# Three weight tiles and the second token mixing's constants, moved into and behind the first chunk of a channel MLP

## The chip, the cores and the metric

The kernel runs on one NeuronCore of a Trainium2 chip. The metric is the device time of one execution in microseconds (us). Times are compared as medians of several runs. The profile is of one further execution.

## What is computed

For 4 batches of 576 tokens with 512 features the reference chains three blocks, all in fp32:

```python
# 1. linear attention, 8 heads of 64
q_p, k_p = phi(q), phi(k)                 # exp(+-(x @ w_phi - max|x @ w_phi|)), 256 features
num = q_p @ (k_p.T @ v); den = q_p @ sum(k_p); x = num / (den + 1e-6)
# 2. first mixer: low-rank token mixing, then a channel MLP of 2048
u = x + (x.T @ U @ V).T                   # U is 576 x 32, V is 32 x 576
x = u + relu(u @ w_ch1) @ w_ch2
# 3. second mixer: token mixing through 256, then a channel MLP of 1536
u = x + (relu(x.T @ w_tok1) @ w_tok2).T
out = u + relu(u @ w_ch1b) @ w_ch2b
```

## The kernel before

Weights arrive as 64-bit floats. `load64` fetches one half of a weight tile (128 x 512) into a ring of raw buffers (L139) and turns it into fp32: two ScalarE activations (L144 for the top word, L145 for the low word) and two VectorE operations (L147 and L150) that put them together. `split` then makes a high part (L96, for these tiles on ScalarE) and a low part (L101, for these tiles on GpSimd). A matrix product is three matmuls: high by high, high by low and low by high (all recorded at L108). The converted half lives in a tile `w` with two buffers, and the low words in `r` with two, so at most two halves are in conversion at once.

The work runs in three stages. Stage A is the attention of all 16 head pairs (`rounds`), with the first mixer's token mixing (`tm0`, `tm1`, `tm2`) and the first 5 of the 16 hidden tiles of the first channel MLP (`ma_u`, `ma_h`, `ma_y`) woven in. Partial results go to DRAM as `uD` (the input of the MLP) and `sD` (the sum so far), in eight chunks of 288 tokens. Stage B takes up these chunks one after the other with the other 11 hidden tiles (`wB`, named b0 to b10, two halves each), and after every second chunk runs the second token mixing (`tokmix2`, with the constants `T1H`, `T1L`, `T2H`, `T2L`). Stage C is the last channel MLP.

`channel` does one chunk. For each hidden tile f, TensorE makes `hp_b` (12 matmuls, `h_tile`), `relu_split` reads it (L185 on ScalarE writes `hhb`, L186 on VectorE writes `hlb`), and `second` adds the product of tile f-1 into four accumulators `yb` (12 matmuls). So TensorE's order is hp 0, hp 1, y 0, hp 2, y 1, hp 3 and so on, and `hp_b` has two buffers.

The order on each engine is settled when the program is built: a scheduler walks the program in its written order with estimated times, and places on each engine's list what is ready, earlier text first. On the chip each engine works through its own list in order. `tc.issue_after(ins)` adds an order edge: of the instructions in its block, those on the engine of `ins` are placed behind it; instructions on other engines are not touched. SyncE (SP) issues all the DMAs.

Before the change, the text after stage A is: load and convert all 11 tiles b0 to b10, load and split the first chunk's input (`u0`, which lives in the space of `T2H` and `T2L`), load and convert the constants of the second token mixing, then the chunks. Tiles b0 to b6 have buffers of their own; b7 to b10 take the buffers of stage A's tiles.

Of the kernel before, what the change touches and what calls it, by code (L numbers as in the profile page):

```python
# [9 lines left out]
F32R = mybir.dt.float32r  # L10
# [9 lines left out]
P = 128  # L20
B = 4
H = 8
S = 576
D = 64
F = 128
# [3 lines left out]
NT = 5  # L29
# [3 lines left out]
NA = 5  # L33
# [2 lines left out]
CHUNKS = (256, 512, 512, 512, 512)  # L36
HM = 256
EARLY = 2


NF32 = 4
WARM = 8


KQB = 6
# [44 lines left out]
def body(ctx, tc, kq, vd, w_phi, U, V, wm1, wt1, wt2, wm2, out):  # L90
# [14 lines left out]
        sub(el, lo, src, f32(hi))  # L105

    def mm(o, l, r, start, stop):
        nc.tensor.matmul(o, l, r, start=start, stop=stop, skip_group_check=True)  # L108

    def group(o, pairs, first=True):  # L110
        n = len(pairs)
# [224 lines left out]
    def k3(g):  # L336
        kvT = a1.tile([P, 2, 2 * F], F32, tag="kvT", name=f"kvT{g}")
        cp("a", kvT, kvps.pop(g))
        tp = psx.tile([P, 4, P], F32, tag="x", name=f"kvt{g}")
        for j in range(2):  # L340
            for s in range(2):
                nc.tensor.transpose(tp[:, 2 * j + s, :], kvT[:, j, s * F : (s + 1) * F], ident)
        if g < NF32:
            KHs[g] = a2.tile([P, 4, P], F32, tag="KH", name=f"KH{g}")
            cp("a", KHs[g], tp)
            return
        KHs[g] = a2.tile([P, 4, P], F32R, tag="KH", name=f"KH{g}")
        KLs[g] = a2.tile([P, 4, P], F32R, tag="KL", name=f"KL{g}")
        split(tp, KHs[g], KLs[g], "a", "v")

    QT = ((0, 1, 4), (2, 3))
    QS = (slice(0, 320), slice(320, S))

# [23 lines left out]
    def q2(g, j, ch):  # L377
        nm = f"{g}_{j}_{ch}"
        n = QS[ch].stop - QS[ch].start
        eh, el = qe.pop((g, j, ch))  # L380
        ps = psx.tile([P, 512], F32, tag="x", name=f"nm{nm}")
        gr = [(KHs[g][:, 2 * j + s], eh[:, s]) for s in range(2)]
        if el is not None:
            gr += [(KLs[g][:, 2 * j + s], eh[:, s]) for s in range(2)]
            gr += [(KHs[g][:, 2 * j + s], el[:, s]) for s in range(2)]
        group(ps[:, :n], gr)
        if ch == 0:
            nds[g, j] = a1.tile([P, S], F32, tag=f"nd{j}", name=f"nd{g}_{j}")
        cp("a", nds[g, j][:, QS[ch]], ps[:, :n])
# [9 lines left out]
    def xr(g):  # L399
        pk = pks.pop(g)  # L400
        with tc.issue_after(subs[-1]):
            nc.vector.tensor_scalar_add(pk, pk, EPS)
        nc.vector.reciprocal(pk, pk)
        rD = drr.tile([2, S], F32, tag="rD", name=f"rD{g}")
        nc.sync.dma_start(rD.rearrange("a (p i) -> (a p) i", i=9), pk)
        rec = a1.tile([P, S], F32, tag="rec", name=f"rec{g}", bufs=RECB)
        nc.sync.dma_start(rec[0:D], rD[0:1].to_broadcast([D, S]))
        nc.sync.dma_start(rec[D:P], rD[1:2].to_broadcast([D, S]))
        recs[g] = rec

    def x1(g):
# [5 lines left out]
            for j, rows in enumerate((slice(0, D), slice(D, P))):  # L417
                nc.vector.tensor_mul(xTs[b][rows, hp, :], nds.pop((g, j))[rows], rec[rows])

    rps = {}  # L420

    def tm0(b, t):
        xT = xTs[b]
        if t == 0:
            rps[b] = psx.tile([P, C], F32, tag="x", name=f"rp{b}")
        rp = rps[b]
        r = P if t < 4 else D
        xp = psx.tile([P, C], F32, tag="x", name=f"xp{b}_{t}")
        for c in range(NC):
            nc.tensor.transpose(xp[:r, c * P : (c + 1) * P], xT[:, c, t * P : t * P + r], ident)  # L430
        xh = at2.tile([P, C], F32R, tag="xh", name=f"xh{b}_{t}")
        xl = at2.tile([P, C], F32R, tag="xl", name=f"xl{b}_{t}")
        split(xp[:r], xh[:r], xl[:r], "a", "v")
        us = US[:r, t].rearrange("p a r -> p (a r)")
        mm(rp, us, xh[:r], t == 0, False)
        mm(rp, us, xl[:r], False, t == NT - 1)

    def tm1(b):
        rh = at2.tile([P, C], F32R, tag="xh", name=f"rh{b}")
# [4 lines left out]
    def tm2(b, ch):  # L444
        rh, rl = rps[b]
        sl = slice(ch * N, (ch + 1) * N)
        xT = xTs[b]
        for c in range(NC):
            mp = psx.tile([P, 512], F32, tag="x", name=f"mp{b}_{ch}_{c}")
            cs = slice(c * P, (c + 1) * P)  # L450
            group(mp[:, :N], [(rh[:, cs], VS[:, sl]), (rl[:, cs], VS[:, sl])])
            nc.vector.tensor_add(xT[:, c, sl], mp[:, :N], xT[:, c, sl])
        nc.sync.dma_start(uD[2 * b + ch], xT[:, :, sl])
# [99 lines left out]
    psg = PB.enter_context(tc.tile_pool(name="psg", bufs=1, space=PSUM, reuse_waits="tile"))  # L553

    nB = NF1 - NA
    wB = [load_w(wrB[f], wm1, NA + f, f"b{f}", f) if f < NR else load_w(wring, wm1, NA + f, f"b{f}") for f in range(nB)]

    def channel(ws, uh, ul, res, o, nm, dst=None, pool=mlp):
        n = uh.shape[2]
        yp = [psy.tile([P, 512], F32, tag=f"y{c}", name=f"y{nm}_{c}") for c in range(NC)]  # L560
        nf = len(ws)

        def second(f, hh, hl):
            wh, wl = ws[f]
            for c in range(NC):
                g = [(w2(wh, c), hh), (w2(wh, c), hl), (w2(wl, c), hh)]
                for i, (l, r) in enumerate(g):
                    mm(yp[c][:, :n], l, r, f == 0 and i == 0, f == nf - 1 and i == 2)

        prev = None  # L570
        for f in range(nf):
            hp = h_tile(psh, ws[f], uh, ul, f"{nm}_{f}")
            hh, hl = h_pair(f, f"{nm}_{f}", pool, n)
            relu_split(hp[:, :n], hh, hl)
            if prev is not None:
                second(*prev)
            prev = (f, hh, hl)
        second(*prev)
        for c in range(NC):
            nc.vector.tensor_add(o[:, c], yp[c][:, :n], res[:, c])  # L580
            if dst is not None:
                nc.sync.dma_start(dst[:, c], o[:, c])

    def tokmix2(b, x2):
        gp = [psg.tile([P, C], F32, tag=f"g{j}", name=f"gp{b}_{j}") for j in range(2)]
        for t in range(NT):
            r = P if t < 4 else D
            xp = psh.tile([P, C], F32, tag="m", name=f"x2p{b}_{t}")
            for c in range(NC):
                nc.tensor.transpose(xp[:r, c * P : (c + 1) * P], x2[:, c, t * P : t * P + r], ident)  # L590
            xh = b2.tile([P, C], F32R, tag="xh", name=f"x2h{b}_{t}")
            xl = b2.tile([P, C], F32R, tag="xl", name=f"x2l{b}_{t}")
            split(xp[:r], xh[:r], xl[:r], "a", "v")
            for j in range(2):
                js = slice(j * P, (j + 1) * P)
                g = [(T1H[:r, t, js], xh[:r]), (T1H[:r, t, js], xl[:r]), (T1L[:r, t, js], xh[:r])]
                for i, (l, rr) in enumerate(g):
                    mm(gp[j], l, rr, t == 0 and i == 0, t == NT - 1 and i == 2)
        gh = bc.tile([P, 2, C], F32R, tag="gh", name=f"gh{b}")
        gl = bc.tile([P, 2, C], F32R, tag="gl", name=f"gl{b}")  # L600
        for j in range(2):
            relu_split(gp[j], gh[:, j], gl[:, j])
        for ch in range(2):
            sl = slice(ch * N, (ch + 1) * N)
            for c in range(NC):
                cs = slice(c * P, (c + 1) * P)
                mp = psy.tile([P, 512], F32, tag=f"y{c}", name=f"m2p{b}_{ch}_{c}")
                g = []
                for j in range(2):
                    g += [(gh[:, j, cs], T2H[:, j, sl]), (gh[:, j, cs], T2L[:, j, sl]), (gl[:, j, cs], T2H[:, j, sl])]  # L610
                group(mp[:, :N], g)
                nc.vector.tensor_add(x2[:, c, sl], mp[:, :N], x2[:, c, sl])
            nc.sync.dma_start(u2D[:, :, b * S + ch * N : b * S + (ch + 1) * N], x2[:, :, sl])
# [6 lines left out]

    u0 = load_u(uD[0], "b0_0", bc, ("T2H", "T2L"))

    T1H = bc.tile([P, NT, 256], F32R, name="T1H")
    T1L = bc.tile([P, NT, 256], F32R, name="T1L")
    for t in range(NT):
        w = load64(wt1[:, t], P, 256, f"t1_{t}")
        split(w, T1H[:, t], T1L[:, t], "v", "v")
    T2H = bc.tile([P, 2, S], F32R, tag="T2H", name="T2H")
    T2L = bc.tile([P, 2, S], F32R, tag="T2L", name="T2L")
    for j in range(2):  # L630
        for k in range(2):
            sl = slice(k * N, (k + 1) * N)
            w = load64(wt2[:, j, sl], P, N, f"t2_{j}_{k}")
            split(w, T2H[:, j, sl], T2L[:, j, sl], "v", "v")

    for b in range(B):
        x2 = b2.tile([P, NC, S], F32, tag="x2", name=f"x2_{b}", bufs=1)
        for ch in range(2):
            nm = f"b{b}_{ch}"
            i = 2 * b + ch  # L640
            _, uh, ul = load_u(uD[i], nm) if i else u0
            xc = x2[:, :, ch * N : (ch + 1) * N]
            nc.sync.dma_start(xc, sD[i])
            channel(wB, uh, ul, xc, xc, nm)
        tokmix2(b, x2)

    BX.close()
    AB.close()
# [275 lines left out]
```

## Time and profile before

| | |
|---|---|
| runs | 1079.35 us median of 3 (1077.38 to 1079.73) |
| the profiled execution | 1074.05 us, of which the span from first to last instruction is 1072.3 us |
| TensorE (PE) busy | 1021.4 us, 95% of the span |
| VectorE (DVE), ScalarE (ACT), GpSimd (POOL) busy | 670.5, 455.5 and 240.4 us |
| chain of work that ended last | PE 75%, DVE 11%, ACT 5%, issue 3%, DMA 3%, POOL 2% |

The chain is followed back from the last instruction, at each step to what released it. PE's busy time counts matmuls that overlap in its pipeline, so a stretch with PE fully busy is one in which matmuls follow each other without a hole, not one at the peak. PEclk is the TensorE clock that was granted, as a share of 2.4 GHz: 1.00 and 0.50 are its two levels, and numbers between them are stretches that hold both.

### The profile page before, as it was taken

How to read it: one execution, taken by the hardware profiler on the slowest of the kernel's cores; microseconds unless marked ns; L12 is line 12 of the kernel's file. 1: busy time of each engine (PE TensorE's matmuls, PEld its weight loads, DVE VectorE, ACT ScalarE, POOL GpSimd, SP SyncE). 2: the span in 40 equal slices, each digit the busy share in tenths (PEclk: the TensorE clock that was granted, in tenths of full speed). 3: DMA queues.
4: the chain of work that ended last, by engine and by line, in shares of the span. 5: the costliest groups of instructions: out<-in, count | busy, mean ns of one | idle time of the engine just before them, and what ended most of it. 6: DMA issues, size and time to landing. Idle time of an engine off the chain costs nothing.

```text
span 1072.3 us, 17821 instructions
## 1 busy us (share of the span) xinstructions
PE 1021.4 (95%) x6960; PEld 948.1 (88%) x6960; DVE 670.5 (63%) x1203; ACT 455.5 (42%) x1067; POOL 240.4 (22%) x186
## 2 busy tenths in 40 slices
PE   8988999899989897999999999999999999999998
PEld 6767899799879787999999999999798988989887
DVE  7888987998898598743223322326898773644533
ACT  6766666756565566532112111114674331312211
POOL 3316556545555234200000000002251000000000
PEclk9999999999999989999999999999999999999999
DMA  7542322232220487520200200111663021030201
GB/s 215 163 148 65 98 69 80 72 98 72 76 79 24 126 276 240 142 79 23 90 23 23 89 23 1 48 42 60 224 204 108 2 83 36 3 116 1 79 1 39
DMA packets 62340, 92.16 MB, mean 86 GB/s; under 512 B 14512, under 2 KB 42928, under 8 KB 62256
## 3 DMA queue, kind: packets, MB, share of 16 engines
q1 hardware_dynamic: 62256, 91.03, 27.0%
q8 instruction: 54, 0.88, 0.3%
q14 instruction: 30, 0.25, 0.1%
HBM read 71.99 MB, written 18.95 MB: 85 GB/s over the span
## 4 chain that ended last, share of the span: by engine, by line
PE 75%; DVE 11%; ACT 5%; issue 3%; DMA 3%; POOL 2%; SPq 0%; DVEq 0%; ACTq 0%; POOLq 0%
PE yc L108 14%; PE yb L108 12%; PE hp_b L108 12%; PE hp_a L108 4%; PE nm L108 4%; PE pp L108 4%; PE kvp L108 4%; PE yp L108 3%; PE vc L108 3%; PE zc L108 3%; PE xc L108 3%; PE gp L108 2%; PE m2p L108 2%; PE dT L361 1%; DMA raw_a<-in_wm_dram 1%
## 5 line engine op out<-in xcount | busy, mean ns | idle before, releaser
L186 DVE SCALAR_TENSOR_TENSOR hlb<-hp_b,hhb 128x288 fp32r<-128x288 f32 x88 | 40.0, 456 | 159.2 <-ACT hhb L185 159.2
L185 ACT ACTIVATE hhb<-hp_b 128x288 fp32r<-128x288 f32 x88 | 36.0, 409 | 202.7 <-PE hp_b L108 199.9
L108 PE MATMUL hp_b<-ulb,wh_b 128*128 128x288 f32 x352 | 104.2, 296 | 0.0
L108 PE MATMUL hp_b<-uhb,wl_b 128*128 128x288 f32 x352 | 104.2, 296 | 0.0
L108 PE MATMUL hp_b<-uhb,wh_b 128*128 128x288 f32 x352 | 104.1, 297 | 0.0
L108 PE MATMUL yb<-hlb,wh_b 128*128 128x288 f32 x352 | 98.3, 299 | 2.3 <-DVE hlb L186 2.1
L101 POOL TENSOR_TENSOR sl<-w_c,sh 128x256 fp32r<-128x256 f32 (+1 forms) x18 | 24.6, 1391 | 329.5 <-ACT sh L96 325.0
L108 PE MATMUL yb<-hhb,wl_b 128*128 128x288 f32 x352 | 97.8, 297 | 0.0
L108 PE MATMUL yc<-hlc,vh 128*128 128x512 f32 (+1 forms) x240 | 88.6, 373 | 0.0
L108 PE MATMUL yc<-hhc,vl 128*128 128x512 f32 (+1 forms) x240 | 88.3, 373 | 0.0
L108 PE MATMUL yc<-hhc,vh 128*128 128x512 f32 (+1 forms) x240 | 81.0, 373 | 0.0
L101 POOL TENSOR_TENSOR qel<-qe,qeh 128x640 fp32r<-128x640 f32 (+1 forms) x48 | 71.4, 1499 | 25.5 <-DVE qeh L98 14.7
L108 PE MATMUL yb<-hhb,wh_b 128*128 128x288 f32 x352 | 68.5, 298 | 4.1 <-ACT hhb L185 4.1
L108 PEld LDWEIGHTS yb<-hlb,wh_b 128*128 128x128 f32 x352 | 66.7, 189 | 3.6 <-DVE hlb L186 3.6
L108 PEld LDWEIGHTS hp_b<-uhb,wh_b 128*128 128x128 f32 x352 | 66.4, 189 | 1.2 <-PE gp L108 1.1
L108 PEld LDWEIGHTS yb<-hhb,wl_b 128*128 128x128 f32 x352 | 66.9, 190 | 0.0
L108 PEld LDWEIGHTS hp_b<-ulb,wh_b 128*128 128x128 f32 x352 | 66.5, 189 | 0.1
L108 PEld LDWEIGHTS hp_b<-uhb,wl_b 128*128 128x128 f32 x352 | 66.3, 188 | 0.0
L293 DVE TENSOR_REDUCE km<-pp 128x4 f32<-128x512 f32 x80 | 54.7, 684 | 14.7 <-PE pp L108 14.2
L101 POOL TENSOR_TENSOR kel<-ke,keh 128x512 fp32r<-128x512 f32 x36 | 48.8, 1366 | 62.4 <-ACT keh L96 60.9
L108 PEld LDWEIGHTS yb<-hhb,wh_b 128*128 128x128 f32 x352 | 54.3, 190 | 4.3 <-ACT hhb L185 4.3
L101 DVE TENSOR_TENSOR kd<-pp,km 128x512 f32<-128x512 f32 x80 | 54.5, 682 | 0.7
(247 smaller groups left out, 3052.1 us busy)
## 6 DMA issues: line engine op xcount, KB each, us to landing
raw_c<-in_wm_dram SPq DMA_DIRECT2D x24, 512.0 KB, 4.5
raw_b<-in_wm_dram SPq DMA_DIRECT2D x22, 512.0 KB, 4.8
kq<-in_kq_dram SPq DMA_DIRECT2D x80, 128.0 KB, 2.2
raw_a<-in_wm_dram SPq DMA_DIRECT2D x10, 512.0 KB, 4.1
rec<-rD SPq DMA_DIRECT2D x32, 144.0 KB, 3.2
uD<-xT SPq DMA_DIRECT2D x8, 576.0 KB, 3.4
sD<-xT SPq DMA_DIRECT2D x8, 576.0 KB, 4.9
x<-sD SPq DMA_DIRECT2D x8, 576.0 KB, 5.3
```

The lines of the kernel that those rows point to most:

```text
L101: return ENG[e].tensor_tensor(out=o, in0=a, in1=b, op=ALU.subtract)
L108: nc.tensor.matmul(o, l, r, start=start, stop=stop, skip_group_check=True)
L185: a = nc.scalar.activation(hh, hp, AF.Relu)
L186: v = nc.vector.scalar_tensor_tensor(out=hl, in0=hp, scalar=0.0, in1=f32(hh), op0=ALU.max, op1=ALU.subtract)
L293: nc.vector.tensor_reduce(out=m, in_=pv, op=ALU.max, axis=AX.X, apply_absolute_value=True)
L361: nc.tensor.transpose(tp[:, o : o + r], ds["q", g, t][:r, j, :], ident[:r, :r])
```

## The change

Tiles b0 to b7 (`READY = 8`) stand where all eleven stood, and their instructions on SP, the 16 loads, are ordered behind the last load of the last reciprocal (`rec`, in `xr`). Tiles b8, b9 and b10 are loaded and converted inside the first chunk: after `relu_split` of hidden tiles 0, 1 and 2, with their ScalarE and VectorE instructions ordered behind those two of that `relu_split`. The constants of the second token mixing are loaded and converted after the first chunk in the text. `keep` would add matmuls, but its two counts are 0, so it adds none.

```diff
+READY = 8
+KEEP_M = 0
+KEEP_Q = 0
...
+    def keep(o, n, behind):
+        r = US.rearrange("p t a r -> p (t a r)")
+        with tc.issue_after(behind):
+            for i in range(n):
+                mm(o, r[:, :P], r[:, :512], i == 0, i == n - 1)
...
-        nc.sync.dma_start(rec[D:P], rD[1:2].to_broadcast([D, S]))
+        recl[:] = [nc.sync.dma_start(rec[D:P], rD[1:2].to_broadcast([D, S])).ins]
...
-    wB = [load_w(wrB[f], wm1, NA + f, f"b{f}", f) if f < NR else load_w(wring, wm1, NA + f, f"b{f}") for f in range(nB)]
+    def load_b(f):
+        if f < NR:
+            return load_w(wrB[f], wm1, NA + f, f"b{f}", f)
+        return load_w(wring, wm1, NA + f, f"b{f}")
+
+    with tc.issue_after(recl[0]):
+        wB = [load_b(f) for f in range(READY)]
...
-        nf = len(ws)
+        nf = nB
...
-            relu_split(hp[:, :n], hh, hl)
+            a, v = relu_split(hp[:, :n], hh, hl)
+            if len(ws) < nB:
+                with tc.issue_after(a), tc.issue_after(v):
+                    ws.append(load_b(len(ws)))
...
-    T1H = bc.tile([P, NT, 256], F32R, name="T1H")
...
+    def mix2_consts():
+        T1H = bc.tile([P, NT, 256], F32R, name="T1H")
...
+        return T1H, T1L, T2H, T2L
...
             channel(wB, uh, ul, xc, xc, nm)
-        tokmix2(b, x2)
+            if i == 0:
+                T1H, T1L, T2H, T2L = mix2_consts()
+        tokmix2(b, x2, T1H, T1L, T2H, T2L)
```

## Rows read from the trace of the kernel before

**Rows 1.** Windows: length; busy of PE, PEld, DVE, ACT, POOL; PEclk, DMA share, GB/s.

```profile
420.00:423.00 3.00, 2.99 (x23) 2.74 (x21) 2.98 (x5) 1.72 (x4) 1.30 (x1) 1.00 0.69 222
423.00:427.10 4.10, 0.00 (x0) 0.00 (x0) 2.93 (x5) 2.74 (x7) 1.54 (x2) 0.77 0.85 265
427.10:432.95 5.85, 5.21 (x23) 4.86 (x24) 4.69 (x6) 3.78 (x7) 2.27 (x2) 0.58 0.73 222
432.95:700.00 267.05, 267.05 (x1947) 261.05 (x1947) 93.96 (x191) 60.34 (x127) 5.17 (x4) 1.00 0.18 55
```

**Rows 2.** Timeline of PE: start, us, instruction, idle time before it and its releaser.

```profile
427.10 1.33 PE L108 MATMUL yb<-hhb,wh_b 128*128 128x288 f32 x4 [4.11 <-ACT hhb L185]
429.07 0.61 PE L108 MATMUL yb<-hlb,wh_b 128*128 128x288 f32 x1 [0.64 <-DVE hlb L186]
...
433.16 0.29 PE L108 MATMUL yb<-hhb,wh_b 128*128 128x288 f32 x1
...
434.76 0.30 PE L108 MATMUL hp_b<-uhb,wh_b 128*128 128x288 f32 x1
```

**Rows 3.** Timeline of ACT around the first chunk's first relu.

```profile
422.45 0.62 ACT L96 CAST wh_b<-w_b 128x512 fp32r<-128x512 f32 x1 [1.03 <-DVE w_b L150]
...
426.62 0.43 ACT L185 ACTIVATE hhb<-hp_b 128x288 fp32r<-128x288 f32 x1
```

**Rows 4.** Timeline of DVE around the first chunk's first relu.

```profile
422.34 0.81 DVE L498 TENSOR_TENSOR xT<-yp,xT 128x288 f32<-128x288 f32 x2
...
427.00 1.65 DVE L150 SCALAR_TENSOR_TENSOR w_b<-raw_b,w_b 128x512 int32<-128x512 int32 x1
428.57 0.44 DVE L186 SCALAR_TENSOR_TENSOR hlb<-hp_b,hhb 128x288 fp32r<-128x288 f32 x1
```

**Rows 5.** Windows of the tile `w_b` alone: two DVE instructions are one half.

```profile
366.00:423.10 57.10, 30.93 (x32) 19.83 (x33) 21.51 (x15) 0.94 0.75 252
423.10:443.10 20.00, 13.09 (x12) 7.16 (x12) 8.98 (x7) 0.83 0.59 175
```

**Rows 6.** Tile `w_b`: count, ns min/median/max, first and last start.

```profile
L144 ACT ACTIVATE w_b<-raw_b x22: 654/668/688, 367.2 to 437.9; 128x512 f32<-128x512 f32 x22
...
L150 DVE SCALAR_TENSOR_TENSOR w_b<-raw_b,w_b x22: 675/692/1774, 369.7 to 439.3; 128x512 int32<-128x512 int32 x22
L96 ACT CAST wh_b<-w_b x22: 603/620/640, 371.5 to 441.1; 128x512 fp32r<-128x512 f32 x22
L101 POOL TENSOR_TENSOR wl_b<-w_b,wh_b x22: 1263/1292/2176, 372.2 to 441.8; 128x512 fp32r<-128x512 f32 x22
```

**Rows 7.** Tile `T1H`: its first use and its conversion.

```profile
L108 PE MATMUL gp<-x2h,T1H x40: 387/437/501, 497.7 to 766.0; 128*128 128x512 f32 x32, 64*128 64x512 f32 x8
...
L101 DVE TENSOR_TENSOR T1L<-w_t,T1H x5: 412/424/426, 444.2 to 450.0; 128x256 fp32r<-128x256 f32 x5
```

**Rows 8.** Tile `T2H`: its first use and its conversion.

```profile
L108 PE MATMUL m2p<-T2H,gh x64: 290/295/398, 511.0 to 779.6; 128*128 128x288 f32 x64
...
L101 DVE TENSOR_TENSOR T2L<-w_t,T2H x4: 447/450/451, 459.3 to 463.6; 128x288 fp32r<-128x288 f32 x4
```

**Rows 9.** Timeline of SP: loads of raw halves.

```profile
71.69 3.32 SPq L139 DMA_DIRECT2D raw_b<-in_wm_dram  x2
...
363.23 0.42 SPq L139 DMA_DIRECT2D raw_b<-in_wm_dram  x1
```

**Rows 10.** DMA issues: us to landing, of the loads issued at 362.18 and 363.23.

```profile
raw_b<-in_wm_dram SPq DMA_DIRECT2D x1, 512.0 KB, 5.0
...
raw_b<-in_wm_dram SPq DMA_DIRECT2D x1, 512.0 KB, 6.5
```

**Rows 11.** Timeline of ACT in the last token mixing of stage A.

```profile
369.38 1.27 ACT L145 ACTIVATE r_b<-raw_b 128x512 int32<-128x512 uint32 x2
370.56 1.06 ACT L96 CAST xh<-xp 128x512 fp32r<-128x512 f32 x2
```

**Rows 12.** Waits of PE from 385 to 420 us: total, times, longest.

```profile
PE yp L108 <- DVE hla L186: 1.2, 2, 0.9
```

More of the change, by code (lines that the diff above doesn't have):

```diff
@@ L107, in mm @@
     def mm(o, l, r, start, stop):
-        nc.tensor.matmul(o, l, r, start=start, stop=stop, skip_group_check=True)
+        return nc.tensor.matmul(o, l, r, start=start, stop=stop, skip_group_check=True)
+    def keep(o, n, behind):
[3 more added lines that the diff above has]
+                mm(o, r[:, :P], r[:, :512], i == 0, i == n - 1)
     def group(o, pairs, first=True):
@@ L341, in k3 @@
             for s in range(2):
-                nc.tensor.transpose(tp[:, 2 * j + s, :], kvT[:, j, s * F : (s + 1) * F], ident)
+                kvl[g] = nc.tensor.transpose(tp[:, 2 * j + s, :], kvT[:, j, s * F : (s + 1) * F], ident).ins
         if g < NF32:
@@ L349, in k3 @@
         split(tp, KHs[g], KLs[g], "a", "v")
+    kvl = {}
     QT = ((0, 1, 4), (2, 3))
@@ L381, in q2 @@
         ps = psx.tile([P, 512], F32, tag="x", name=f"nm{nm}")
+        if g == NF32 - 1 and j == 0 and ch == 0:
+            keep(ps, KEEP_Q, kvl[g])
         gr = [(KHs[g][:, 2 * j + s], eh[:, s]) for s in range(2)]
@@ L418, in x1 @@
                 nc.vector.tensor_mul(xTs[b][rows, hp, :], nds.pop((g, j))[rows], rec[rows])
-    rps = {}
+    rps, rpl, recl = {}, {}, []
     def tm0(b, t):
@@ L435, in tm0 @@
         mm(rp, us, xh[:r], t == 0, False)
-        mm(rp, us, xl[:r], False, t == NT - 1)
+        rpl[b] = mm(rp, us, xl[:r], False, t == NT - 1).ins
     def tm1(b):
@@ L450, in tm2 @@
             cs = slice(c * P, (c + 1) * P)
+            if c == 0 and ch == 0 and b == 0:
+                keep(mp, KEEP_M, rpl[b])
             group(mp[:, :N], [(rh[:, cs], VS[:, sl]), (rl[:, cs], VS[:, sl])])
@@ L582, in channel, with tokmix2 @@
                 nc.sync.dma_start(dst[:, c], o[:, c])
-    def tokmix2(b, x2):
+    def tokmix2(b, x2, T1H, T1L, T2H, T2L):
         gp = [psg.tile([P, C], F32, tag=f"g{j}", name=f"gp{b}_{j}") for j in range(2)]
@@ L621, in body @@
     u0 = load_u(uD[0], "b0_0", bc, ("T2H", "T2L"))
-    T1H = bc.tile([P, NT, 256], F32R, name="T1H")
[L624 to L634, printed above, removed]
+    def mix2_consts():
+        T1H = bc.tile([P, NT, 256], F32R, name="T1H")
+        T1L = bc.tile([P, NT, 256], F32R, name="T1L")
+        for t in range(NT):
+            w = load64(wt1[:, t], P, 256, f"t1_{t}")
+            split(w, T1H[:, t], T1L[:, t], "v", "v")
+        T2H = bc.tile([P, 2, S], F32R, tag="T2H", name="T2H")
+        T2L = bc.tile([P, 2, S], F32R, tag="T2L", name="T2L")
+        for j in range(2):
+            for k in range(2):
+                sl = slice(k * N, (k + 1) * N)
+                w = load64(wt2[:, j, sl], P, N, f"t2_{j}_{k}")
+                split(w, T2H[:, j, sl], T2L[:, j, sl], "v", "v")
+        return T1H, T1L, T2H, T2L
     for b in range(B):
```

## The prediction

> **What bounds the kernel now.** I read the page first: the end is set by TensorE's own stream, so a change counts only where it closes a hole in that stream or moves the granted clock. Then I looked for holes around the change with the windows. From 432.95 to 700 us PE is busy for the whole 267.05 us at clock 1.00 [rows 1]: whatever is moved into that stretch costs nothing as long as it opens no hole, and a microsecond gained before it moves everything behind it forward. Just before it lies the one place that the change touches. From 420 to 423 us PE is full, from 423.00 to 427.10 it does nothing, and from 427.10 to 432.95 it works at a mean clock of 0.58 [rows 1].
>
> The timeline tells what ends the hole. PE has made hp 0 and hp 1 of the first chunk and now needs `hhb` of tile 0: it waits 4.11 us for it, does four matmuls, and waits 0.64 us more for `hlb` [rows 2]. The relu itself takes 0.43 us on ACT and 0.44 us on DVE. It is late because of what stands ahead of it on the two lists: ACT starts it only at 426.62, DVE at 428.57, right behind an L150 of a weight half [rows 3, 4]. The windows of `w_b` alone say which halves these are: up to 423.1 us there are 32 DVE instructions, that is 16 halves, exactly b0 to b7; the other 6 halves, b8 to b10, follow in the next 20 us [rows 5]. So the first chunk's first relu stands behind conversions of b8 and b9, which no matmul needs for another 20 us.
>
> **The change, part by part.**
>
> *The relu's place.* With b8 ordered behind the relu of tile 0 on both engines, the last conversion left ahead of it on ACT is the cast of b7's second half. That cast runs from 422.45 to 423.07 [rows 3]; with its 0.43 us the relu then ends at 423.5. On DVE the list ahead ends with two additions of stage A, 422.34 to 423.15 [rows 4], so `hlb` can run from 423.5 to about 423.95. PE runs dry at 423.0 [rows 1], so I leave a hole of 0.5 us. The four matmuls that need `hhb` alone, 0.53 us at the pace of 12 in 1.60 us [rows 2], then cover the wait for `hlb`. Of 4.11 + 0.64 = 4.75 us of waiting, 4.2 us go. Bounds: all 4.75 go if the relu slips ahead of b7's cast; 2.9 go if two activations of b8, 0.67 us each [rows 6], still stood ahead. I take 4.2, because the order edge covers all ACT and DVE instructions of b8.
>
> *The clock.* After the hole, 24 matmuls run from 427.10 to the start of y 1 at 433.16 us, 6.06 us with the 0.64 us wait in them; the next 12, at clock 1.00, take 434.76 - 433.16 = 1.60 us [rows 2]. At that pace the 24 would take 3.2 us, so the lower level of the clock costs 6.06 - 0.64 - 3.2 = 2.2 us. The engine had been idle for 4.11 us before. With a hole of 0.5 us I expect the clock to stay up: the nearest row is a hole of 0.9 us between 385 and 420 us [rows 12], and from 420 to 423 the clock still stood at 1.00 [rows 1]. Bounds: 0 (it falls anyway) and 2.2; I take 2.2. Sum of both terms: 4.2 + 2.2 = 6.4 us.
>
> *b8 to b10 inside the chunk.* 6 halves, each with two activations (0.67 us each, taking L145 like L144) and a cast (0.62) on ACT, 1.29 us on POOL [rows 6] and two DVE operations of 1.0 us on average (44.0 us in 44 [rows 5]): 5.2 us from end to end, and a new one every 20 / 6 = 3.3 us [rows 5]. Started at 423.9, b8 is whole at 423.9 + 3.3 + 5.2 = 432.4, b9 at 439.0, b10 at 445.6, its first half at 442.3. A step of the chunk (12 matmuls of hp, 12 of y) takes 3.2 us at the pace above, so with y 0 at 423.5, hp 8 starts at 423.5 + 1.6 + 6 x 3.2 = 444.3, hp 9 at 447.5, hp 10 at 450.7. The least cover is that of b10's first half, 8.4 us. Cost nothing; if that cover were gone, PE would wait for b10 by what is missing. Their 6 loads carry no edge on SP and keep their place in the ring of raw buffers, since the order b0 to b10, then constants, is the old one.
>
> *The constants.* Nine pieces move behind the chunk in the text. Before, T1's last split started at 450.0 and its first use at 497.7; T2's at 463.6 and 511.0 [rows 7, 8]. Both have 47 us of cover. T2 had to wait for `u0`'s space before as well. A few us later costs nothing.
>
> *The edge behind `rec`.* Two raw loads were issued at 71.69, some 290 us before the others; the third of the others was issued at 363.23 [rows 9]. With the edge these two join the burst behind `rec`. By the ring of raw buffers they are the halves of b1 (13 halves are loaded before b0, and of every five the first two use the ring that stage A has too), so they become third and fourth. Rows give landings of 362.18 + 5.0 = 367.2 for the first and 363.23 + 6.5 = 369.7 for the third [rows 10], so 1.3 us apiece and about 371.0 for the fourth. The first ACT instruction on b1 is the second of the two L145 from 369.38, so near 370.0 [rows 11]: 0.3 us after landing. Behind it on ACT stand casts `xh` of the last token mixing, which PE waits for. Bounds: a loss of 2.3 us if b1 landed as late as the fifth (372.3), a gain of 0.6 us if that L145 moves behind the `xh` casts. I take 0. The Trainium skill ("DMA: Bandwidth & Descriptors", Rules for kernel authors) says to issue a transfer early and wait on it late, which speaks against this edit; by that rule the early issue hid something and the sum would be 6.4 - 2.3 = 4.1 us, against 6.4 by the rows.
>
> *Nothing:* `keep` with counts of 0, and `nf = nB`, which is the same 11.
>
> **From the profiled execution to the runs.** It took 1074.05 us, 1.75 us of it outside the span; 6.4 less is 1067.65. The median of the runs is 5.3 us above it, and I take the saving off the median: 1079.35 - 6.4 = **1073.0 us**. About 0.2%, 2.2 us, is what a measurement of this kernel can tell from no change.
>
> **Rivals.**
>
> *The relu waits for something else.* The constants' conversions carry no edge, and the scheduler could fill ACT and DVE with them, or with the second chunk's input, where b8 stood. For it: the relu was placed by estimated times, and these had it late. Against it: b8 to b10 come first in the ring of raw buffers, so the constants have no buffer before b8 is converted. The hole would stay: 1079 us.
>
> *Half the gain.* The clock falls all the same (4.2 us saved, 1075.2 us), with two activations of b8 ahead as well (2.9 saved, 1076.5 us), or b1 lands late (6.4 - 2.3 = 4.1 saved, 1075.3 us). For the first speaks that the clock was at its lower level behind the only long hole here, against it that the hole shrinks to an eighth.
>
> *A looser stage A.* With the two early loads gone, the scheduler places the casts of the last token mixing ahead of conversions. Four `xh` casts stand behind an L145 or L144 of 0.67 us there at most once each, so up to 2.7 us: 1070.3 us.
>
> *Slower: relus of the first chunk held up at every step.* Where conversions and relus were mixed in stage A, PE waited for a relu (`hla`) twice, by up to 0.9 us [rows 12]; the list of DVE also held L150s there, of 0.69 us at the median and up to 1.77 [rows 6]. If each of the 10 later relus of the chunk cost 0.9 us, that is 9 us against 6.4 gained: 1082.0 us. The sign turns at 0.64 us a step. Against it: b9's last halves and b10 were mixed with relus after 432.95 already, and PE shows no hole there [rows 1], as a relu has 3.2 us until its product is due. The Trainium skill ("SBUF — State Buffer", § SBUF: two separate sides) has VectorE operations with two SBUF inputs and GpSimd operations that read SBUF exclude each other for a whole instruction. By that rule each L150 that meets the POOL subtraction is 1.1 us longer; at 10 steps it would be 11 us lost and 1084 us. The trace agrees on the length (1.77 against 0.69), not on any wait of PE in this stretch.
>
> **How the numbers follow.** As forecast (1071 to 1074.5): 0.58. Half the gain: 0.15, of it 0.04 for late b1. Looser stage A: 0.08. Relu waits for something else: 0.11. Slower: 0.08, of it 0.03 at the longer price. Faster by over 0.2%: 0.58 + 0.15 + 0.08 = 0.81; same 0.11; slower 0.08. The range from 1069.5 to 1079.2 leaves out the slower case, half of the unchanged one and a little of the lower one, 0.17 in all.
>
> **What would show it.** Right: `hhb` of tile 0 on ACT right behind the 16th `wh_b` cast; PE's wait for it under 1 us; PEclk 1.00 from 420 to 440; the 17th to 22nd `wh_b` casts after it and before 450 us; no wait of hp 8 to hp 10; T1 and T2 done well before 490. Wrong: a wait of `yb` or `hp_b` in tiles 1 to 10, a fall of the clock near 425, `xh` casts of the last token mixing waiting for a raw load, or a span that moves by other than the sum because the scheduler rearranged stage A, where two loads left the list at 71.69.

## The result, and the profile after

The changed kernel takes 1068.47 us at the median of 7 runs (1065.8 to 1072.49), the kernel before 1079.73 us beside it (7 runs, 1075.58 to 1083.54): ratio 0.9908, 95% interval 0.9885 to 0.9931. A second comparison on another occasion gave 0.9926 (0.9905 to 0.9947). The forecast of faster holds; the forecast time of 1073.0 us is 4.5 us too long, and the measured one lies 1.0 us below the lower end of the range. One execution of the kernel before (1405.55 us) and one of the filled kernel below (2524.1 us) were disturbed and are left out of every time here. The profiled execution took 1067.35 us, its span 1065.6 us against 1072.3: 6.7 us less, close to the 6.4 of the sum. So two questions are left: whether these 6.7 us come from where the sum has them, and where the rest of the 9 to 11 us between the medians is.

The page of the changed kernel gives busy time with share of the span, and the chain that ended last, by engine:

```profile
PE 1020.9 (96%) x6960; PEld 947.8 (89%) x6960; DVE 668.1 (63%) x1203; ACT 455.7 (43%) x1067; POOL 239.3 (22%) x186
...
PE 70%; DVE 14%; ACT 5%; DMA 4%; issue 4%; POOL 2%; SPq 0%; DVEq 0%; POOLq 0%; ACTq 0%
```

The work is the same and PE is still the bound. The same four windows as [rows 1], of the changed kernel:

```profile
420.00:423.00 3.00, 3.00 (x25) 3.00 (x24) 1.96 (x6) 2.96 (x6) 1.30 (x1) 1.00 0.57 132
423.00:427.10 4.10, 4.10 (x33) 4.10 (x32) 2.66 (x6) 3.77 (x8) 2.33 (x2) 1.00 0.49 180
427.10:432.95 5.85, 5.85 (x46) 5.85 (x45) 4.43 (x5) 3.40 (x7) 1.86 (x3) 1.00 0.85 280
432.95:700.00 267.05, 266.52 (x1935) 259.58 (x1934) 91.95 (x189) 58.80 (x124) 3.81 (x3) 1.00 0.17 54
```

The stretch that had no matmul has 33, and the clock, 0.77 and 0.58 before, is 1.00. Only the last window is worse than in [rows 1]: PE lacks 0.53 us in it. The timelines of ACT and of DVE show the relu of tile 0 where the forecast put it, and three later relus, of tiles 4, 5 and 6, that are late:

```profile
420.04 0.63 ACT L100 CAST wh_b<-w_b 128x512 fp32r<-128x512 f32 x1 [1.96 <-DVE w_b L160]
420.56 0.41 ACT L195 ACTIVATE hhb<-hp_b 128x288 fp32r<-128x288 f32 x1
420.87 0.67 ACT L154 ACTIVATE w_b<-raw_b 128x512 f32<-128x512 f32 x1
...
436.25 0.41 ACT L195 ACTIVATE hhb<-hp_b 128x288 fp32r<-128x288 f32 x1
...
440.60 0.45 ACT L155 ACTIVATE r_t<-raw_t 128x256 int32<-128x256 uint32 x1 [1.35 <-DVE w_t L157]
440.95 0.42 ACT L154 ACTIVATE w_t<-raw_t 128x256 f32<-128x256 f32 x1
441.27 0.40 ACT L195 ACTIVATE hhb<-hp_b 128x288 fp32r<-128x288 f32 x1
```

```profile
421.00 0.46 DVE L196 SCALAR_TENSOR_TENSOR hlb<-hp_b,hhb 128x288 fp32r<-128x288 f32 x1 [0.27 <-ACT hhb L195]
...
433.40 1.32 DVE L157 SCALAR_TENSOR_TENSOR w_b<-w_b,r_b 128x512 int32<-128x512 int32 x1 [1.26 <-ACT w_b L154]
434.64 0.45 DVE L196 SCALAR_TENSOR_TENSOR hlb<-hp_b,hhb 128x288 fp32r<-128x288 f32 x1
...
436.54 1.73 DVE L160 SCALAR_TENSOR_TENSOR w_b<-raw_b,w_b 128x512 int32<-128x512 int32 x1
438.19 0.44 DVE L196 SCALAR_TENSOR_TENSOR hlb<-hp_b,hhb 128x288 fp32r<-128x288 f32 x1
439.28 1.29 DVE L157 SCALAR_TENSOR_TENSOR w_t<-w_t,r_t 128x256 int32<-128x256 int32 x1 [0.65 <-ACT w_t L154]
```

420.04 is the cast of b7's second half, the 16th of 22; `hhb` of tile 0 follows it, at 420.56 where [rows 3] have 426.62, and b8 follows `hhb`. Further down, `hlb` of tile 4 stands behind an L157 of b10, that of tile 5 behind an L160 of b10 that takes 1.73 us, and `hhb` of tile 6 behind two conversions of the constants, the first of which (L155) waits for the L157 from 439.28. PE's timeline shows what each does:

```profile
421.47 0.69 PE L112 MATMUL yb<-hhb,wh_b 128*128 128x288 f32 x4
422.00 0.29 PE L112 MATMUL yb<-hlb,wh_b 128*128 128x288 f32 x1
...
434.17 0.69 PE L112 MATMUL yb<-hhb,wh_b 128*128 128x288 f32 x4
435.14 0.40 PE L112 MATMUL yb<-hlb,wh_b 128*128 128x288 f32 x1 [0.29 <-DVE hlb L196]
...
437.91 0.68 PE L112 MATMUL yb<-hhb,wh_b 128*128 128x288 f32 x4
438.69 0.40 PE L112 MATMUL yb<-hlb,wh_b 128*128 128x288 f32 x1
...
441.72 0.80 PE L112 MATMUL yb<-hhb,wh_b 128*128 128x288 f32 x4
442.57 0.40 PE L112 MATMUL yb<-hlb,wh_b 128*128 128x288 f32 x1
```

Where [rows 2] have waits of 4.11 and 0.64 us, y 0 follows hp 1 with none, and its first `hlb` matmul starts 0.53 us after its first matmul. In y 4, y 5 and y 6 the same distance is 0.97, 0.78 and 0.85 us, and y 6 starts 0.39 us after the last hp matmul in place of 0.13. Matmuls overlap, so only one of these delays is listed as idle time; it is the distance between starts that tells the loss. From y 4 to y 5 and from y 5 to y 6 it is 3.74 and 3.81 us, where the kernel before takes 3.18 for a step.

For this reason all kernels below are compared by the starts of the same matmuls. The table is worked out from such starts in the PE timelines, plus that of `x1` on DVE (us, from "to mp" on each since the column before; the names are those of the experiments below; "last x1": first of the last two multiplications L431 of stage A; mp: first of the second half of the last token mixing of stage A, which is that of the last batch; hp 0, y 1: of the first chunk; gp: of the first batch; hpc: the first hidden tile of stage C, near 760; before_look are two more executions of the kernel before):

```
kernel            edge  last x1  to mp  to hp 0  to y 1  to gp  to hpc  to end
before             no    364.1   12.21   43.33   13.56   64.57  269.65  304.89
before_look_1      no    362.0   14.02   43.75   14.29   64.58  269.76  306.22
before_look_2      no    368.8   13.36   43.64   14.21   64.57  269.72  306.06
fill               no    363.2   12.67   42.68   12.64   67.70  269.81  304.90
no_rec_edge        no    361.9   13.66   42.63    7.08   66.47  269.83  306.11
no_rec_again       no    364.5   13.51   42.60    7.11   66.73  269.77  306.09
all_eleven_ahead   yes   362.7   14.03   42.08   13.03   64.56  269.80  306.01
text_only          yes   362.9   13.79   41.78   13.25   64.56  270.13  306.05
after              yes   362.8   13.66   41.83    6.37   66.21  269.81  304.91
after_again        yes   362.3   12.52   41.80    6.37   66.30  269.78  304.89
consts_edge        yes   366.5   14.08   42.02    6.37   65.54  269.92  304.94
ready6             yes   361.6   14.00   41.78    6.37   69.21  269.69  304.97
xh_first           yes   370.8   12.60   45.62    6.37   65.71  269.64  306.15
```

From hp 0 to y 1 the change saves 13.56 - 6.37 = 7.19 us; from y 1 to gp it gives 1.64 us back. Ahead of hp 0 it saves 1.33 us (419.61 to 418.28); from gp on, nothing.

### The profile page after: what moved, and what is told of

It reads as the page before. It is cut to its first block, busy times and chain, and to the rows that moved or that the text cites. A ratio compares the mean times of both kernels' runs of the same rounds, so it can differ in the third digit from the quotient of the medians.

```text
span 1065.6 us, 17826 instructions
## 1 busy us (share of the span) xinstructions
PE 1020.9 (96%) x6960; PEld 947.8 (89%) x6960; DVE 668.1 (63%) x1203; ACT 455.7 (43%) x1067; POOL 239.3 (22%) x186
## 4 chain that ended last, share of the span: by engine, by line
PE 70%; DVE 14%; ACT 5%; DMA 4%; issue 4%; POOL 2%; SPq 0%; DVEq 0%; POOLq 0%; ACTq 0%
PE yc L112 14%; PE yb L112 11%; PE hp_b L112 11%; PE hp_a L112 4%; PE yp L112 3%; PE pp L112 3%; PE vc L112 3%; PE zc L112 3%; PE xc L112 3%; PE kvp L112 3%; PE gp L112 2%; PE nm L112 2%; PE m2p L112 2%; PE dT L372 2%; DVE xT L431 1%
## 5 line engine op out<-in xcount | busy, mean ns | idle before, releaser
L112 PEld LDWEIGHTS hp_b<-ulb,wh_b 128*128 128x128 f32 x352 | 66.2, 188 | 0.1
L112 PEld LDWEIGHTS yb<-hhb,wl_b 128*128 128x128 f32 x352 | 66.3, 188 | 0.0
L112 PEld LDWEIGHTS hp_b<-uhb,wl_b 128*128 128x128 f32 x352 | 66.2, 188 | 0.0
## 6 DMA issues: line engine op xcount, KB each, us to landing
uD<-xT SPq DMA_DIRECT2D x8, 576.0 KB, 3.5
sD<-xT SPq DMA_DIRECT2D x8, 576.0 KB, 5.0
x<-sD SPq DMA_DIRECT2D x8, 576.0 KB, 5.1
```

What stands on the lines that cost most here:

```text
L112: return nc.tensor.matmul(o, l, r, start=start, stop=stop, skip_group_check=True)
```

## The experiments

The theory is the forecast's: the saving comes from the order of the first chunk's relus against b8 to b10, and the edge behind `rec` is worth nothing. The first rival says that the place in the text already does it, the second that the edge behind `rec` does it, or a part of it.

**Without the edge behind rec.** The loads of b0 to b7 go free again; all else is the change.

```diff
-    with tc.issue_after(recl[0]):
-        wB = [load_b(f) for f in range(READY)]
+    wB = [load_b(f) for f in range(READY)]
```

> The change without the order edge behind rec, so that two raw halves are loaded near 72 us again. Theory (the relu's place makes the gain, the edge behind rec about 1.3 us of it through stage A): no hole at the first relu, ratio to before 0.990 to 0.995, span 1066 to 1068. Rival (the edge behind rec makes the gain): ratio 0.997 to 1.002.

Measured: 1072.48 us, ratio 0.9941 (0.992 to 0.9961). So the hole goes without this edge, and the other part of the change is worth 5 to 6 us. PE and ACT around y 0, in the second execution of this kernel that was profiled (no_rec_again, below):

```profile
424.41 0.80 PE L112 MATMUL yb<-hhb,wh_b 128*128 128x288 f32 x4 [0.44 <-ACT hhb L195]
```

```profile
423.42 0.62 ACT L100 CAST wh_b<-w_b 128x512 fp32r<-128x512 f32 x1 [1.95 <-DVE w_b L160]
423.95 0.40 ACT L195 ACTIVATE hhb<-hp_b 128x288 fp32r<-128x288 f32 x1
```

Here is nearly the forecast's picture: `hhb` right behind the 16th cast, a hole of 0.44 us (the forecast left 0.5), and no fall of the clock behind it (PEclk 1.00 in every window from 420 to 440 us). What the changed kernel has beyond this is the edge behind `rec`.

**The edge behind rec alone.** All eleven tiles ahead of the chunk, as before; the edge stays, and the constants stay behind the chunk in the text.

```diff
-READY = 8
+READY = 11
```

> The change with all 11 tiles ahead of the first chunk again: what is left of it is the loads ordered behind rec and the constants behind the chunk. Theory (the first relu's place makes the gain): the first relu stands behind the 17th cast as before, the hole of about 4 us and the slow matmuls behind it come back, 7 us of the gain are lost; ratio to before 0.997 to 1.002, span 1070 to 1073. Rival (the edge behind rec, by rearranging stage A, makes the gain): ratio 0.990 to 0.993, and the span stays near 1066.

Measured: 1075.51 us, ratio 0.9969 (0.9955 to 0.9982), just below the 0.997 to 1.002 expected: 3.3 us by the ratio (1.9 to 4.8; the medians are 2.1 us apart). The order of every engine's instructions in this kernel is the same as with the constants back at their old place in the text (seen in the two programs; the second was not run), so moving them in the text does nothing by itself and the 3.3 us are the edge's. Its timeline of PE has the hole again:

```profile
426.08 1.33 PE L112 MATMUL yb<-hhb,wh_b 128*128 128x288 f32 x4 [3.93 <-ACT hhb L195]
```

**The place in the text alone.** b8 to b10 stand inside the chunk in the text, but without the order edges behind the relus.

```diff
             if len(ws) < nB:
-                with tc.issue_after(a), tc.issue_after(v):
-                    ws.append(load_b(len(ws)))
+                ws.append(load_b(len(ws)))
```

> The change with b8 to b10 written inside the first chunk but without the two order edges behind each relu. Theory (the order edge is what puts the relu ahead, the place in the text alone does not): the first relu still stands behind the 17th cast, the hole comes back, ratio to before 0.997 to 1.002, span 1070 to 1073. Rival (the place in the text does it, since earlier text goes first): relu behind the 16th cast, no hole, ratio 0.990 to 0.993.

Measured: 1074.51 us, ratio 0.9975 (0.9954 to 0.9996), the ratio of the `rec` edge alone within the intervals. ACT, and then PE, of this kernel:

```profile
420.23 0.62 ACT L100 CAST wh_b<-w_b 128x512 fp32r<-128x512 f32 x1 [1.03 <-DVE w_b L160]
...
423.93 0.61 ACT L100 CAST wh_b<-w_b 128x512 fp32r<-128x512 f32 x1
...
425.36 0.39 ACT L195 ACTIVATE hhb<-hp_b 128x288 fp32r<-128x288 f32 x1
```

```profile
425.80 1.33 PE L112 MATMUL yb<-hhb,wh_b 128*128 128x288 f32 x4 [3.94 <-ACT hhb L195]
```

The relu is behind the 17th cast again and PE waits 3.94 us. PE's list is the same as in the changed kernel; those of ACT and DVE differ. That shows the first rival wrong: the scheduler places by its estimated times, and the edges alone overrule it.

**The kernel before, unchanged (before_again).**

> The kernel before once more, for a second profile. The profiled execution of before was 5.3 us faster than the median of its runs. Theory (executions differ in how long the granted clock is at its lower level): its mean granted clock is below 0.988 when its span is above 1072, the hole at the first relu is again 4 to 5 us, and the difference of spans lies in stretches whose clock differs. Rival (executions differ in the hole itself): the hole is 6 us or more in a slower execution.

Measured: 1078.16 us at the median of nine, ratio 0.9996 (0.9979 to 1.0013), which is how well a comparison tells no change. What was asked of a second profile is answered by the two further executions below.

**The hole filled.** The kernel before, with 30 more matmuls behind hp 1 of the first chunk; nothing reads their result.

```diff
+FILL = 30
...
+            if nm == "b0_0" and f == 1:
+                fp = psg.tile([P, C], F32, tag="g0", name="fill")
+                with tc.issue_after(lastmm[0]):
+                    for i in range(FILL):
+                        mm(fp[:, :n], w1(ws[0][0], i % NC), uh[:, i % NC, :], i == 0, i == FILL - 1)
```

> The kernel before with one thing added: 30 extra matmuls of 128x288 into a PSUM bank that nothing reads, put in PE's list right behind hp 1 of the first chunk, where before has 4.11 us without a matmul. The relu stays where it was, behind the 17th cast, so the order of the work is that of before. It asks whether the hole costs only its own length or also the clock behind it. Clock theory (a term of 2.2 us in the forecast's sum): the hole's time is as before, or some tenths longer, since 30 matmuls at about 0.13 us are 3.9 us against a hole of 4.11; but the granted clock stays 1.00 from 420 to 433, so that y 0 ends where it did, hp 3 to y 2 run at the higher level, and gp of the first batch is 1.5 to 2.5 us earlier than before's 497.7; the time falls by about 2 us, ratio 0.998. Rival: the clock falls for a reason that lies ahead of the hole, or not at this place; then nothing changes, or the time rises by what the 30 matmuls overrun the hole.

Measured: 1079.0 us at the median of eleven, ratio 1.001 (0.9994 to 1.0026): the 2 us expected did not come. Windows around the filled hole, then PE there, then PE's waits from 418 to 500 us (total, times, longest):

```profile
423.00:427.10 4.10, 3.30 (x23) 2.85 (x22) 3.45 (x4) 2.98 (x6) 1.64 (x2) 1.00 1.03 323
427.10:432.95 5.85, 4.93 (x37) 4.93 (x38) 4.67 (x7) 3.61 (x6) 2.21 (x2) 1.00 0.71 227
```

```profile
421.75 4.15 PE L109 MATMUL fill<-uhb,wh_b 128*128 128x288 f32 x30
426.06 0.40 PE L109 MATMUL yb<-hhb,wh_b 128*128 128x288 f32 x1 [0.16 <-ACT hhb L188]
428.02 0.40 PE L109 MATMUL yb<-hlb,wh_b 128*128 128x288 f32 x1 [1.56 <-DVE hlb L189]
```

```profile
PE yb L109 <- DVE hlb L189: 2.2, 2, 1.6
PE yb L109 <- ACT hhb L188: 1.1, 2, 0.9
```

The clock stays at 1.00, so it had fallen behind the idle time, as the forecast read it. But y 1 comes only 0.9 us earlier, since a faster PE waits 1.56 us for `hlb` where the slow one waited 0.64, and after y 1 the chunk takes 3.1 us more: at full clock PE runs into the relus of the next tiles, which are still behind conversions. The 2.2 us of the clock are not a gain by themselves. They can be had only together with relus that come earlier.

**Five tiles in place of three inside the chunk.**

```diff
-READY = 8
+READY = 6
```

> The changed kernel with five tiles (b6 to b10) in place of three converted inside the first chunk. It tests the forecast's working for the cover: tile f's first half is ready at 423.9 + 6.6 (f - READY) + 5.2 us and wanted at 425.1 + 3.2 (f - 2). With 8 tiles ahead the least cover is 8.4 us (b10, here 442.3 against 450.7); with 6 ahead the relu goes up behind the 12th cast, still without a hole, and b10 is ready at 455.5, some 4.8 us late, b9 1.4 us late. So by this working hp 9 and hp 10 wait, the chunk ends about 4 to 5 us later than with 8, and the time is 3 to 5 us above the changed kernel's, ratio to before about 0.995. Rival: the raw tiles and conversions take less than 6.6 us apiece when they aren't behind one another (DVE has room in the chunk), so that nothing waits and the time is the changed kernel's within 0.5 us. Second rival: the relus themselves are held up in all of tiles 0 to 5, and the time is 5 us or more above.

Measured: 1071.23 us, ratio 0.9938 (0.9914 to 0.9962), some 3 us above the changed kernel; hp 0 to gp takes 75.58 us against 72.58. The size is a little under the 4 to 5 us expected for the chunk, but the mechanism is another. PE's waits from 417 to 493 us:

```profile
PE yb L112 <- DVE hlb L196: 1.0, 3, 0.6
PE yb L112 <- ACT hhb L195: 0.7, 2, 0.4
PE yb L112 <- DVE x L604: 0.2, 1, 0.2
```

No hp waits for a weight. What waits is y, for relus that conversions hold up: five tiles cost through the relus before they cost through lateness of a tile. By the starts of the groups only 1.1 of the 3.0 us more lie in the first chunk; 1.9 us lie ahead of and in y 0 of the second, where the constants' conversions, which come later here, stand ahead of the relu.

**The constants behind the whole chunk.** The changed kernel, with the constants' ACT and DVE instructions ordered behind the chunk's last relu.

```diff
+            last[:] = a, v
...
-                T1H, T1L, T2H, T2L = mix2_consts()
+                with tc.issue_after(last[0]), tc.issue_after(last[1]):
+                    T1H, T1L, T2H, T2L = mix2_consts()
```

> The changed kernel with the constants of the second token mixing ordered behind the last relu of the first chunk on ScalarE and VectorE, instead of right behind that chunk in the text alone. In the changed kernel's profile the steps of tiles 3 to 5 lose about 1.6 us against the step of 3.18, and some of the constants' instructions stand between the relus there. If these are what holds the relus back, the steps of tiles 4 and 5 go back to 1.59 us a group, gp of the first batch comes 0.5 to 1.2 us earlier than the changed kernel's 490.85, and the time falls by as much (ratio to before 0.990). Rival: the conversions of b8 to b10, which stand between the relus by the change's own edges, hold them back; then the 1.6 us stay and the time is the changed kernel's within 0.3 us. Against both: the constants are late for the first token mixing and gp waits, by more than 1 us.

(The tiles called 3 to 5 there are 4 to 6, counted as here.) Measured: 1068.28 us, ratio 0.9904 (0.9881 to 0.9928): not told apart from the changed kernel. In the trace y 1 to gp is 65.54 us in place of 66.21, within the 0.5 to 1.2 us earlier that were expected; the waits from 422 to 500 us are down to tile 4's:

```profile
PE yb L112 <- DVE hlb L196: 0.4, 1, 0.4
```

By the starts of the groups the steps of tiles 5 and 6 are as short as in the kernel before, which gives 1.07 us back; tile 4 still loses 0.67; and y 0 of the second chunk now loses 0.36, with conversions of the constants ahead of its `hlb`. So of the 1.64 us the constants' place in the first chunk costs 1.07, a third of which the edge only moves into the second chunk, and b8 to b10 by themselves cost 0.6 to 0.7.

**The last token mixing ahead of the conversions.** The changed kernel, with b0 to b7 ordered behind the first `xh` and `xl` of that mixing, so that `xh` no longer stands on ACT behind conversions that wait for a raw load.

```diff
+        xsp[b, t] = split(xp[:r], xh[:r], xl[:r], "a", "v")
...
-    with tc.issue_after(recl[0]):
+    xa, xv = xsp[B - 1, 0]
+    with tc.issue_after(recl[0]), tc.issue_after(xa), tc.issue_after(xv):
```

> The changed kernel with the loads and conversions of b0 to b7 ordered also behind the first xh and xl conversions of the last token mixing, on ScalarE and VectorE. In the changed kernel rp of batch 0 waits 3.3 us for xh, which stands on ScalarE behind conversions of b0 that wait for their raw tile's landing at 366.6. Theory that stage A's end is set by that wait: rp starts 2 to 3 us earlier, at about 366, the clock does not fall at that place, and hp_b 0 comes 1 to 3 us earlier than 418.28, if the eight tiles then still come in time; the time falls by 1 to 3 us. Rival one: what follows rp on the chain (its own chain of tiles, the second half of the mixing, the write and reading back of u) waits for something else, so that hp_b 0 stays within 0.5 us: same time as the changed kernel. Rival two: the conversions come so much later that the eight tiles are late for the first chunk and hp or y of its last tiles wait: slower by what they wait, 1 us or more.

(The `rp` called batch 0's there is the last batch's.) Measured: 1073.88 us, ratio 0.9948 (0.9931 to 0.9966): 5 us slower than the changed kernel. The profiled execution is the slowest of its eight (1078.64 us), so its clock need not be that of the others. The first `rp` starts 2.6 us after the last x1 in place of 5.6, as expected, but hp 0 comes later, not earlier: mp to hp 0 takes 45.62 us in place of 41.83. Windows of this kernel from 378 us:

```profile
378.00:384.00 6.00, 4.95 (x9) 2.54 (x10) 4.99 (x8) 4.82 (x10) 2.83 (x2) 0.51 0.55 199
384.00:395.00 11.00, 9.74 (x39) 9.05 (x39) 9.49 (x17) 7.63 (x12) 4.79 (x4) 0.50 0.77 228
```

and of the changed kernel in the same places of its order, which come some 8 us earlier:

```profile
370.00:376.00 6.00, 5.33 (x19) 3.29 (x17) 4.67 (x8) 5.29 (x11) 2.57 (x2) 0.80 0.63 216
376.00:387.00 11.00, 8.58 (x40) 7.76 (x40) 11.00 (x17) 6.72 (x11) 4.61 (x3) 0.69 0.72 214
```

PE is at 1.2 GHz for nearly the whole 17 us here. The theory behind this experiment is not borne out: of the 3 us by which `rp` starts earlier 1.1 are left at mp (12.60 against 13.66 us), and more than that is lost behind it, where the clock is low. Whether an earlier `rp` would bring hp 0 earlier at the same clock is not shown, nor why the clock stays low for longer. Neither rival names this.

**Two more executions of the kernel before.**

> The kernel before, unchanged, for one more profiled execution. Its executions take 1073 to 1083 us and the one in the document 1074.05, near their fast end. Theory: the slower executions have the same order and the same hole of the first chunk (hp_b 0 to y 1 in 13.0 to 13.6 us), and what they lose lies ahead of the first chunk, in the first 100 us and in the stretches where the granted clock is at its lower level, so that first batch's gp to the end takes 844.5 us (1072.3 less 497.7 is 574.5) within 1.5 us and from the third x1 on the kernel differs by 2 us at most. Rival: the first chunk itself differs from execution to execution, with a hole of 8 us or more in some, in which case the change is worth more than 6 to 7 us in those.

> As before_look_1: one more profiled execution of the kernel before, unchanged. The theory and its rival are the same: hp_b 0 to y 1 takes 13.0 to 13.6 us here too, and what is longer than in the profile shown lies ahead of the first chunk or in stretches at the lower clock; or, by the rival, the hole itself differs.

(The 844.5 in the first is a slip; 574.5 is meant.) Measured: 1076.41 and 1082.69 us, spans 1074.6 and 1080.4. The part from gp to the end is 576.0 and 575.8 us, as expected. The hole is the same, 4.10 and 4.09 us, so the rival falls. hp 0 to y 1, 14.2 to 14.3 us, is longer than the 13.0 to 13.6 given, by 0.7 us than in the profile on which the forecast rests; all of it lies in hp 2, behind the hole, which ran at the lower level of the clock for longer (2.77 and 2.69 us against 2.01). Of the 2.3 and 8.1 us by which their spans are longer, 0.2 and 6.2 lie ahead of hp 0, 0.7 each between hp 0 and y 1, and 1.4 and 1.2 behind gp. The 2 us allowed from the third x1 on are exceeded (4.2 and 4.5).

**The edge behind rec, sized.** The changed kernel and the one without that edge again, in one comparison.

> The changed kernel again, beside the next one on the same chip, to size the edge behind rec. Theory that the edge is worth some 3 us (the kernel with that edge alone had ratio 0.9969 to before; the changed kernel without it 0.9941, with it 0.9908): ratio 0.988 to 0.993 here, 2 to 4 us below no_rec_again. Rival (the forecast's own: the edge costs and gains nothing): both within 1 us of each other, near ratio 0.9925. In its profile hp_b 0 to y 1 is 6.4 us and hp_b 0 to gp of the first batch 72.6, as in the changed kernel's first profile.

> The changed kernel without the edge behind rec, again. By the theory that the edge is worth some 3 us: ratio 0.9925 to 0.996, 2 to 4 us above after_again. By the rival: within 1 us of after_again. In its profile hp_b 0 to y 1 is 6.4 to 7.1 us; the way from the last x1 to hp_b 0, where the tiles of the main part are loaded, shows whether the edge shortens it (55.5 us in the changed kernel, 56.3 without the edge, 55.5 in the kernel before).

Measured: 1067.89 us, ratio 0.9926 (0.9905 to 0.9947), and 1071.85 us, ratio 0.9946 (0.9928 to 0.9964): 4.0 us apart, though the intervals overlap. Over both comparisons the medians are 1068.4 us (13 executions) and 1072.2 us (12), 3.8 us apart. With the 3.3 us of the edge alone that is two kinds of comparison of one sign and size. PE's waits from 385 to 418 us, first without the edge, then with it:

```profile
PE yp L112 <- DVE hla L196: 1.2, 2, 0.9
```

```profile
PE yp L112 <- DVE hla L196: 0.6, 1, 0.6
```

The wait of [rows 12] stands unchanged in both profiles of the changed kernel without the edge, and is 0.6 us or none in after, after_again, all_eleven_ahead and text_only.

## Why the prediction was right, and where it was off

*The relu's place*: right. 4.2 us were expected with a hole of 0.5 us left; without the edge behind `rec` the hole left is 0.44 us, with it none.

*The clock*: right that it stays up and that the 24 matmuls then run at full pace: from hp 0 to y 1 the chunk loses 6.9 us without the edge (mean of the three executions before, 14.02, to 7.10) and 6.8 with it (13.14 to 6.37). The two terms made 6.4. The filled hole adds that the 2.2 us hold only as long as relus keep up with a PE at full clock.

*b8 to b10 inside the chunk* and *The constants*, "cost nothing": failed, by 1.7 us (64.56 to 66.2 and 66.3 with the edge) or 2.0 (64.57 to 66.5 and 66.7 without). The cover was worked out rightly: no hp waits, the 17th to 22nd casts start from 424.08 to 438.30 us, the last pieces of T1 and T2 at 447.1 and 456.7, and even five tiles inside leave cover enough. What was left out of this step is that the conversions stand on ACT and DVE between the relus. This is the mechanism of the rival *Slower: relus of the first chunk held up at every step*. It acts in three steps, tiles 4 to 6, not in ten (a wait of `yb` there was among its signs of being wrong), and costs 0.57, 0.37 and 0.70 us there. Each of the three relus has an operation ahead of it on DVE that runs into a subtraction of POOL and lasts longer for it:

```profile
432.88 1.30 POOL L105 TENSOR_TENSOR wl_b<-w_b,wh_b 128x512 fp32r<-128x512 f32 x1 [1.28 <-ACT wh_b L100]
436.42 1.29 POOL L105 TENSOR_TENSOR wl_b<-w_b,wh_b 128x512 fp32r<-128x512 f32 x1 [2.25 <-ACT wh_b L100]
439.00 1.29 POOL L105 TENSOR_TENSOR wl_b<-w_b,wh_b 128x512 fp32r<-128x512 f32 x1 [1.28 <-ACT wh_b L100]
```

POOL ends at 434.18, 437.71 and 440.29 us. The L157 from 433.40 (1.32 us), the L160 from 436.54 (1.73) and the constants' L157 from 439.28 (1.29) end 0.3 to 0.6 us behind these ends; apart from POOL the first two take 0.69 us and the third 0.42. That agrees with the rule of the Trainium skill ("SBUF — State Buffer", § SBUF: two separate sides) that a VectorE operation with two SBUF inputs and a GpSimd operation that reads SBUF exclude each other for a whole instruction. At the shorter times all three relus would have been ready for their matmuls: an estimate from these starts, as no run takes POOL's work away. In the kernel before, the L150 of 1.65 us of [rows 4] delayed `hlb` of tile 0 in this way (POOL from 426.82 to 428.10); behind 432.95 us [rows 1] none held up a matmul.

*The edge behind `rec`*, "I take 0", with bounds from a loss of 2.3 to a gain of 0.6 us: this is the step that failed most, by 3.3 to 3.8 us. The working for the loads was right: the two raw loads of b1 join the burst,

```profile
360.94 3.09 SPq L149 DMA_DIRECT2D raw_b<-in_wm_dram  x5
```

and their first conversion on ACT that [rows 11] had ahead of `xh` is behind it, the bound on the side of a gain. The Trainium skill's rule ("DMA: Bandwidth & Descriptors", Rules for kernel authors) to issue early and wait late would have had the edit cost something; no run here shows that it did. But the working looked only at the loads. The edge changes the order that the scheduler writes: between no_rec_again and after, 20 instructions of PE, 16 of ACT and 11 of DVE stand at another place (by the program's names in the traces), all of them in the last 50 us of stage A. It was the prediction's own last item under "Wrong" (a span that moves because the scheduler rearranged stage A). The rival *A looser stage A* had the sign and, with 2.7 us, nearly the size, but not the place: from the last x1 to mp nothing is gained (12.2 to 14.0 us without the edge, 12.5 to 14.1 with it). The gain that comes back in each profile is from mp to hp 0, 42.6 to 43.8 us without the edge and 41.8 to 42.1 with it (xh_first apart), where the waits for `hla` shrink or go. Further, the 16th cast ends earlier against hp 0 by 1.1 us, which closes the last hole at y 0 (7.1 to 6.4 us). That is 0.5 to 2.0 us and 0.7 us.

Together: -6.9 at the hole, +1.7 to +2.0 in tiles 4 to 6, and -1.2 to -2.7 from the edge make -6.1 to -7.9 us. The errors of two steps cancel almost fully against the profiled execution, -6.7 us; that its difference agrees with 6.4 is in part luck.

*From the profiled execution to the runs*: the medians are 9.4 us apart over all comparisons (1077.8 us in 58 executions of the kernel before in the later comparisons, 1068.4 in 13 of the changed one). A straight line through each kernel's times over the mean granted clock of its executions gives 1076.1 and 1069.5 us at the same clock of 0.986, 6.6 us apart; the median clock is 0.9825 before and 0.987 after, 0.0045 apart. But 6.6 us is too low for the change, since the change itself raises the mean clock: in [rows 1] the hole and the stretch behind it lack 0.23 x 4.10 + 0.42 x 5.85 = 3.4 us of clock, 0.0032 of the span. Taken along either line between clocks that differ by these 0.0032, the difference is 8.2 to 8.6 us (an estimate). About 1 us is left that goes with the clock elsewhere, mostly ahead of hp 0, where it differs between executions of one kernel; and up to 2.5 us between this and the sum by places is not settled.

## What to carry to other kernels

Where an engine's list is written by estimated times, an instruction that the bound engine waits for can stand behind work that nobody needs yet: look at what precedes it on its list, and order the later work behind it, since moving that work in the text may change nothing. What is put between urgent instructions is not free because its own due time is far; ask what each piece delays on the list that it joins. And an order edge on loads can be worth as much through the order that it makes the scheduler write elsewhere as through the loads, so an edge that "does nothing" is to be measured alone.

## What the runs showed of the hardware

The same short hole was followed by a lower clock in some executions and not in others. Behind the first hpc, near 765 us, PE has two waits, 0.6 us for `gh` and 0.8 us for `u1c`, in all 13 profiles of the table alike. Windows there, of after_again and then of no_rec_again:

```profile
761.00:764.00 3.00, 2.18 (x18) 1.94 (x17) 3.00 (x4) 2.06 (x5) 3.00 (x3) 1.00 0.60 212
764.00:767.00 3.00, 3.00 (x26) 3.00 (x26) 2.93 (x6) 2.60 (x5) 0.11 (x1) 1.00 0.79 266
```

```profile
764.00:767.00 3.00, 1.94 (x11) 1.39 (x10) 2.97 (x3) 3.00 (x8) 3.00 (x3) 1.00 0.69 218
767.00:770.00 3.00, 2.54 (x12) 2.54 (x13) 2.97 (x5) 1.15 (x2) 2.25 (x2) 0.60 0.72 227
```

It costs 1.2 us (304.9 against 306.1 in the table's last column) and was met in 7 of 13 profiles; executions of the kernel before stand on both sides. One profile of each of two kernels can differ by as much for this reason alone. And a PE kept busy with 30 matmuls that nothing reads held the clock at 1.00 but gained no time (ratio 1.001).
